# Sparse attention and a gated feed-forward on one core: 64-row value tiles with a VectorE halo copy, one cast queue in order of need, block means by row sums, score halves joined

## The chip, the core and the metric

The kernel runs on one core of one Trainium2 chip. The metric is the device time of one execution in microseconds (us). Several executions of both kernels are made alternately on the same chip. One execution is recorded by the hardware profiler. "Span" below is the time from the first to the last instruction of that recorded execution.

A ratio is the mean time of one kernel's fast runs over the mean time of the other's fast runs from the same rounds, so it is not quite the ratio of the medians that are quoted beside it. A run counts as slow when it is more than 1.5% above the fastest of the same kernel. A ratio below 1 means faster than the kernel before. A profile, and with it a span, is of one run only.

## The reference, cut to what matters

There are 4 batches, 8 heads, 768 positions and 64 values a head. Every query sees its neighbours at a distance below 16, and 24 blocks of 32 keys, each summarised by the maximum of its keys and the mean of its values. A feed-forward with a sigmoid gate follows.

```python
k_sum = k.reshape(B, H, nb, block, D).max(axis=3)        # block = 32, nb = 24
v_sum = v.reshape(B, H, nb, block, D).mean(axis=3)
scores_l = scale * q @ k.T                               # kept where |i - j| < 16
scores_s = scale * q @ k_sum.T + np.log(block)
a = softmax(concat([scores_l, scores_s]))
x = a @ concat([v, v_sum])                               # (B*S, 512) for the feed-forward
out = (sigmoid(x @ w_gate) * (x @ w_val)) @ w_out        # 512 -> 1536 -> 512
```

The kernel works in bf16 with fp32 sums.

## The kernel before

Each query tile has 64 queries. Its keys are 96 neighbours (rows 0 to 95 of a value tile) and the 24 block summaries (rows 96 to 119), so one product of 120 rows makes both parts. The value tiles of neighbouring query tiles overlap by 32 rows, and each is loaded whole:

```python
def load_v(b, t0, t1):
    for t in range(t0, t1):
        lo, hi = max(0, QT * t - 16), min(S, QT * t + 80)          # up to 96 rows
        ...
        nc.gpsimd.dma_start(out=vx_t[b % 2][r0:r0 + hi - lo, t, :, 0:64], in_=v[b, :, lo:hi, :]...)
```

For batches 0 and 1 the block means are 12 matmuls against a band of 1/32. For batches 2 and 3 they come from separately loaded block rows that GpSimd adds in halves:

```python
def V(self, *_):                                   # batches 0 and 1, on TensorE
    vsp = ps([128, 512], FP32, "vsp")
    for t in range(NQ):
        nc.tensor.matmul(out=vsp[96:128]..., lhsT=zband[:, 30 - 2 * t:62 - 2 * t],
                         rhs=vx[0:W, t, :, 0:64], start=(t == 0), stop=(t == NQ - 1))
    ...
    nc.scalar.copy(out=vx[96:120, 0, :, 0:64], in_=src)    # batch 1
    self.replicate(t0)                                     # one DMA copies it to the other tiles

def L(self, g, h=None): ...       # block rows, [96, 2048] fp32, on the sync queue
def R(self, g, h=None): ...       # GpSimd: sum of the 32 rows by halves
def M(self, g, h=None): ...       # GpSimd: times 1/32, then a small DMA into vx[96:120, 0]
```

Loads use three paths. Keys and queries of batches 0 and 1 come in fp32 on the queues of SyncE and ScalarE and are cast by an engine. Values, weights and the later batches come through GpSimd's queue, which casts while it copies. Attention work of the next batch is spread in between the feed-forward units of the current one:

```python
REST = "Q0 Q1 S0b Q2 S1b Q3 S2b S3b A0b A1b X0b A2b X1b A3b X2b X3b"
FIRST = "T0 T1 S0a S0b T2 S1a S1b T3 S2a S2b V S3a S3b"            # batch 1
LAST = "- - A0 A1 X0 A2 X1 A3 X2 X3"
spread(m1[0][1:], a0.units(REST), 2, 10)
extra = (att[1].units(FIRST) + [lambda: loads(2), lambda: means(2)]
         + att[1].units(LAST) + att[2].units(FIRST_KEYS))
spread(m1[1] + ffn.units2(), extra, 4, 23)
```

Here T and Q transpose keys and queries, S makes scores, V the block means, A the products with the values, and X transposes the result into the feed-forward's input.

The softmax here doesn't subtract the row's maximum and nothing guards it: scores larger than these inputs give would overflow.

## Time and profile before

| | kernel before |
|---|---|
| median (lowest to highest) | 256.43 us (254.42 to 256.79) |
| span of the profiled run | 251.1 us |
| TensorE, VectorE, ScalarE, GpSimd busy | 92%, 47%, 43%, 45% |
| first gapless feed-forward unit of batch 0 | 28.14 us |
| second half of batch 0's first layer | 48.17 us |
| second layer of batch 0 | 73.85 us |
| feed-forward of batch 1 | 94.01 us |

The last four rows are start times read from the engine time line; they cut the run into stages.

### The profile page before, as it was taken

To read this page: it belongs to the slowest core of one execution; us is meant where nothing else is said; L and a number is where in the kernel's file an instruction comes from. 1 tells how busy PE (TensorE), PEld (TensorE's weight loads), DVE (VectorE), ACT (ScalarE), POOL (GpSimd) and SP (SyncE) were. 2 spreads that over 40 slices of the span, in tenths; PEclk is the share of its full clock that TensorE was granted. 3 is DMA by queue.
4 is the path that set the end of the run, shared out by engine and by line. 5 is a ranking of instruction groups with operands and counts; after the bars stand their busy time and mean duration, and the time that the engine had idled before them with its cause. 6 is when DMAs were issued, how large, how long until landed. Compare 5 with 4: busy or idle time off the path is not lost.

```text
span 251.1 us, 5090 instructions
## 1 busy us (share of the span) xinstructions
PE 230.2 (92%) x2020; PEld 130.3 (52%) x2032; DVE 119.2 (47%) x243; ACT 107.8 (43%) x193; POOL 111.7 (45%) x151
## 2 busy tenths in 40 slices
PE   1696899599999999799999999999999999999993
PEld 1473566366544556455554455555544465655441
DVE  5876348247833412976563208766543034444000
ACT  2862476239943344445631134645511243333121
POOL 8998276489998389994069930000000000000000
PEclk9999999999999999999999999999999999999999
DMA  6999999999999999999999965600024310000122
GB/s 220 238 158 162 226 270 287 263 189 142 124 122 170 225 221 145 193 171 206 176 121 163 197 171 132 113 13 3 0 76 147 117 42 0 4 0 0 57 112 84
DMA packets 100687, 34.27 MB, mean 136 GB/s; under 512 B 84496, under 2 KB 97208, under 8 KB 100280
## 3 DMA queue, kind: packets, MB, share of 16 engines
q0 software_dynamic: 70720, 12.46, 65.7%
q1 hardware_dynamic: 28856, 20.70, 33.5%
q10 hardware_dynamic: 1088, 0.79, 1.0%
q8 instruction: 16, 0.26, 0.4%
q14 instruction: 7, 0.06, 0.1%
HBM read 34.34 MB, written 6.29 MB: 162 GB/s over the span
## 4 chain that ended last, share of the span: by engine, by line
PE 71%; DMA 17%; POOL 6%; issue 2%; DVE 1%; ACT 1%; SPq 0%; POOLq 0%; ACTq 0%; DVEq 0%
PE m L414 22%; PE gp L397 21%; PE vp L397 21%; DMA wv<-in_moe_w_val_dram 11%; POOL vx L166 3%; DMA kTn<-nat 3%; PE sc L257 2%; PE av L340 2%; DMA vx<-vx 2%; PE vsp L280 1%; PE tp L197 1%; POOL wg L174 1%; DVE kTx L233 1%; PE br L368 1%; POOL wv L174 1%
## 5 line engine op out<-in xcount | busy, mean ns | idle before, releaser
L405 DVE SCALAR_TENSOR_TENSOR hT<-gate,vp 128x384 bf16<-128x384 f32 x96 | 52.8, 551 | 68.9 <-PE vp L397 65.0
L397 PE MATMUL vp<-xT,wv 128*128 128x384 bf16 x384 | 78.6, 326 | 4.2 <-DMA wv<-in_moe_w_val_dram 2.7
L397 PE MATMUL gp<-xT,wg 128*128 128x384 bf16 x384 | 78.8, 327 | 1.1 <-ACT xT L371 1.1
L404 ACT ACTIVATE gate<-gp 128x384 f32<-128x384 f32 x96 | 47.4, 494 | 51.4 <-DVE hT L405 42.9
L414 PE MATMUL m<-wo,hT 128*128 128x512 bf16 x276 | 64.3, 379 | 0.6
L397 PEld LDWEIGHTS <-wv 128*128 128x128 bf16 x384 | 37.5, 98 | 30.6 <-issue 3.1
L397 PEld LDWEIGHTS <-wg 128*128 128x128 bf16 x384 | 35.3, 98 | 22.1
L414 PEld LDWEIGHTS <-hT 128*128 128x128 bf16 x288 | 26.9, 98 | 30.7
L166 POOL DMA_DIRECT2D vx<-in_v_dram x48 | 37.0, 800 | 13.1 <-PE sc L257 9.0
L419 ACT ACTIVATE ot<-m 128x512 f32<-128x512 f32 x24 | 14.3, 597 | 52.1 <-PE m L414 51.9
L263 ACT ACTIVATE P<-sc 128x768 bf16<-128x768 f32 x32 | 26.0, 815 | 12.3 <-PE sc L257 12.2
L264 DVE TENSOR_TENSOR P<-P,mask 128x768 bf16<-128x768 bf16 x32 | 17.8, 555 | 14.1 <-ACT P L263 13.9
L311 POOL TENSOR_TENSOR vm<-vm 96x1024 f32<-96x1024 f32 (+4 forms) x20 | 20.4, 1020 | 5.8 <-DMA vm<-in_v_dram 4.4
L233 DVE TENSOR_REDUCE kTx<-kTn 128x24 bf16<-128x768 bf16 x16 | 15.2, 949 | 4.5 <-ACT kTn L203 2.5
L349 DVE TENSOR_TENSOR xs<-av,rec 128x768 bf16<-128x768 f32 (+1 forms) x20 | 15.9, 797 | 0.7
L197 PE MATMUL tp<-ident,qkbf 128*128 128x128 bf16 x96 | 8.9, 253 | 6.9 <-DVE qkbf L120 5.9
L257 PEld LDWEIGHTS <-kTx 64*128 64x128 bf16 x384 | 7.9, 97 | 11.8 <-issue 8.5
L347 DVE RECIPROCAL rec<-av 128x12 f32<-128x12 f32 (+1 forms) x20 | 4.3, 215 | 19.9 <-PE av L340 19.8
L257 PE MATMUL sc<-qT,kTx 64*128 64x64 bf16 x384 | 12.0, 196 | 1.9 <-DVE kTx L237 1.2
L156 POOL DMA_DIRECT2D nat<-in_q_dram x16 | 13.2, 894 | 0.4 <-issue 0.4
L122 POOL CAST qkbf<-nat 128x768 bf16<-128x768 f32 (+1 forms) x12 | 8.5, 723 | 11.0 <-DMA nat<-in_q_dram 7.6
L156 POOL DMA_DIRECT2D nat<-in_k_dram x16 | 13.3, 852 | 0.1
(50 smaller groups left out, 114.0 us busy)
## 6 DMA issues: line engine op xcount, KB each, us to landing
out_dram<-ot SPq DMA_DIRECT2D x24, 256.0 KB, 4.6
vx<-in_v_dram POOLq DMA_DIRECT2D x40, 96.0 KB, 5.4
vm<-in_v_dram SPq DMA_DIRECT2D x4, 768.0 KB
vm<-in_k_dram SPq DMA_DIRECT2D x4, 384.0 KB, 6.9
nat<-in_k_dram SPq DMA_DIRECT2D x4, 384.0 KB
nat<-in_q_dram SPq DMA_DIRECT2D x4, 384.0 KB, 13.9
wo<-in_moe_w_out_dram POOLq DMA_DIRECT2D x6, 256.0 KB, 16.2
nat<-in_k_dram POOLq DMA_DIRECT2D x16, 96.0 KB, 4.2
```

The lines of the kernel that those rows point to most:

```text
L156: nc.gpsimd.dma_start(out=nat[:, h // 2, :, 64 * (h % 2):64 * (h % 2) + 64], in_=tap[b, h].rearrange("(c p) d -> p c d", p=128))
L166: nc.gpsimd.dma_start(out=vx_t[b % 2][r0:r0 + hi - lo, t, :, 0:64], in_=v[b, :, lo:hi, :].transpose([1, 0, 2]))
L233: nc.vector.tensor_reduce(out=kTx[:, 0, W:KX], in_=kTn[:, 16:16 + S].rearrange("p (n w) -> p n w", w=32), axis=AX.X, op=ALU.max)
L257: nc.tensor.matmul(out=sc[:, i, QT * t6:QT * (t6 + 1)], lhsT=kTx[64 * i:64 * i + 64, t, :], rhs=qT[64 * i:64 * i + 64, QT * t:QT * (t + 1) ...
L263: nc.scalar.activation(out=Ph, in_=sc[:, :, 0:6 * QT], func=ACT.Exp, scale=SCALE)
L264: nc.vector.tensor_tensor(out=Ph, in0=Ph, in1=mask[:, None, 6 * hf:6 * hf + 6, :].rearrange("p i t w -> p i (t w)") .to_broadcast([128, 2, ...
L311: nc.gpsimd.tensor_tensor(out=st[:, 0:n], in0=st[:, 0:n], in1=st[:, n:2 * n], op=ALU.add)
L349: nc.vector.tensor_tensor(out=xs[:, 0:3 * G].rearrange("p (g a) i d -> p g (a i) d", g=G), in0=avf[:, :, :, 0:64], in1=rec[:, 0:G].to_broa ...
L397: nc.tensor.matmul(out=o, lhsT=wb[:, c, 128 * f:128 * (f + 1)], rhs=self.xT[:, c, HALF * hf:HALF * (hf + 1)], start=(c == 0), stop=(c == N ...
L404: nc.scalar.activation(out=gate, in_=gp, func=ACT.Tanh, scale=0.5)
L405: nc.vector.scalar_tensor_tensor(out=self.hT[hf][:, f, :], in0=gate, scalar=1.0, in1=vp, op0=ALU.add, op1=ALU.mult)
L414: nc.tensor.matmul(out=self.m3, lhsT=self.hT[hf][:, f, 128 * tt:128 * (tt + 1)], rhs=wo_bf[:, f], start=(f == 0), stop=(f == NF - 1))
```

## The change

Its intent is to take load off the transfer engines and TensorE: value tiles of 64 rows (a third fewer bytes), the missing 32 rows copied by VectorE from the next tile; casting done by the queue, and the loads of batches 0 and 1 on one queue in the order in which they are needed, so that weights do not compete with later batches (the first-half queries of batch 0 still come in fp32 on SyncE's queue and are cast by VectorE, and the block rows of batches 2 and 3 stay on SyncE's queue too); batch 1's block means by VectorE sums of loaded rows; the near products of batch 0 taken before its block means are known; and both halves of a score pair made together.

```diff
 def load_v(b, t0, t1):
-            lo, hi = max(0, QT * t - 16), min(S, QT * t + 80)
+            lo, hi = max(0, QT * t - 16), min(S, QT * t + (48 if t < NQ - 1 else 80))
+        def halo(self, t0, t1):
+            nc.vector.tensor_copy(out=self.vx[64:96, t0:t1], in_=self.vx[0:32, t0 + 1:t1 + 1])
+        def G(self, g, h=None):                      # batch 1: row sums on VectorE
+            sm = vm_pool.tile([4 * NS, 64], FP32, name="sm", tag="sm")
+            nc.vector.tensor_reduce(out=sm, in_=st.rearrange("p (w d) -> p d w", w=32), axis=AX.X, op=ALU.add)
-        def B(self, *_):
-            self.replicate(1)                        # a DMA
+        def B(self, g, h=None):                      # VectorE
+            t0, t1 = (1, 6) if g == 0 else (6, NQ)
+            nc.vector.tensor_copy(out=self.vx[96:120, t0:t1], in_=self.vx[96:120, 0:1]...)
 ... (near, recips, far: batch 0's first half in two products)
+    load_gates((0, 1), (1, 1), (2, 2))
+    for p in range(NP):
+        srcs[0][p].append(load_qk(nc.gpsimd, q, 0, p, rows(3), half=1))
+    load_gates((4, 2), (6, 2), (8, 2), (10, 2))
+    srcs[1][0], srcs[1][1] = load_nat(1)
+    for i in range(6):
+        load_wo(i)
+    for g in range(2):
+        att[1].L(g, queue=nc.gpsimd)
+    load_v(1, 0, NQ)
 ...
+    NEXT = """
+        4 T0   5 T1   6 Z0   7 T2   8 Z1   9 T3   10 Z2   12 Z3 G0 M0   13 G1 M1   15 H0 H1   17 B0 B1
+        18 A0 A1   19 A2 A3 X0   20 X1   21 X2   22 X3"""
+    at.setdefault(4, []).append(lambda: loads(2))
+    at.setdefault(14, []).append(lambda: block_rows(2))
```

Z is both halves of a score pair, H the halo copies, G the row sums; the numbers are the feed-forward units after which the work is put out.

## The prediction

> **What bounds the kernel now.** I read the page first (shares, slices), then the chain that ended last, then the time line of the engines that it names, then the DMA queues in short windows.
>
> ```profile
> PE 230.2 (92%) x2020; PEld 130.3 (52%) x2032; DVE 119.2 (47%) x243; ACT 107.8 (43%) x193; POOL 111.7 (45%) x151
> ...
> DMA  6999999999999999999999965600024310000122
> ...
> PE 71%; DMA 17%; POOL 6%; issue 2%; DVE 1%; ACT 1%; SPq 0%; POOLq 0%; ACTq 0%; DVEq 0%
> ```
>
> TensorE is busy 92% of 251.1 us, and no other compute engine reaches half. But the DMA row (busy tenths of the 16 transfer engines) is full for nearly all of the first 23 of 40 slices, some 144 us: there are two resources to fill here, and transfers need not be late to be close to it. The third line is the chain: 23% of it lies on transfers and on GpSimd (POOL), nearly all of it early. Its longest piece, with its start and length:
>
> ```profile
> 25.31 21.82 DMA wv<-in_moe_w_val_dram
> ```
>
> The last slice of one weight, issued at 25.31, takes 21.82 us to land, and TensorE waits for it. TensorE's time line (start, length, instruction, count, in brackets the idle time before and what ended it) has the stages that the change touches:
>
> ```profile
> 28.14 0.81 PE L397 MATMUL gp<-xT,wg 128*128 128x384 bf16 x4
> ...
> 47.18 0.82 PE L397 MATMUL vp<-xT,wv 128*128 128x384 bf16 x4 [2.69 <-DMA wv<-in_moe_w_val_dram]
> ...
> 70.87 2.76 PE L280 MATMUL vsp<-vx,zband 96*32 96x512 bf16 x12
> ...
> 79.52 0.25 PE L340 MATMUL av<-vx,P 120*64 120x65 bf16 x2
> ...
> 94.01 0.81 PE L397 MATMUL gp<-xT,wg 128*128 128x384 bf16 x4
> ...
> 102.86 0.81 PE L397 MATMUL vp<-xT,wv 128*128 128x384 bf16 x4 [1.53 <-DVE hT L405]
> ```
>
> The feed-forward of batch 0 runs without gaps from 28.14, waits 2.69 us for weights, then makes block means of batch 1 by matmul (2.76 us), reaches batch 1's value products at 79.52 and batch 1's feed-forward at 94.01. From there to the end (251.1) TensorE is nearly always busy: 157.1 us. GpSimd in that time:
>
> ```profile
> 60.85 6.59 POOL L156 DMA_DIRECT2D nat<-in_k_dram  x8
> 67.37 6.63 POOL L156 DMA_DIRECT2D nat<-in_q_dram  x8
> 73.86 6.24 POOL L166 DMA_DIRECT2D vx<-in_v_dram  x8
> 80.89 3.02 POOL L166 DMA_DIRECT2D vx<-in_v_dram  x4 [0.79 <-DMA vx<-in_v_dram]
> ```
>
> Issuing the 28 loads of batch 2 holds GpSimd for 23 us, 0.83 us for a key or query load and 0.77 for a value tile, and nothing that TensorE waits for stands behind them. That last point is what the change alters.
>
> **What the Trainium skill says.** "DMA: Bandwidth & Descriptors", section "SWDGE vs HWDGE vs iDMA": a transfer that casts can only be issued from GpSimd, where software makes its descriptors. The trace agrees on the cost: every cast load takes 0.72 to 0.94 us of GpSimd, almost whatever its size (0.72 for a wo slice of 256 packets, 0.77 for a value tile of 768). Same page, "Issuing engines are not separate DMA queues": all queues share the same 16 engines, so one queue instead of three gains order and not bandwidth; the full DMA row beside three queues fits. "TensorE: Matmul & The Clock Gate", Part 1: TensorE falls to half clock after about 3.4 us of idleness and needs as much work to come back. The trace shows it at the start: 16 filler matmuls took 1.47 us at 14.6 and 1.07 us at 17.1. "VectorE: DVE Perf Modes", the tier table: a bf16 copy in SBUF moves four elements a cycle. It agrees: 1152 elements took 0.45 us at 8.5, so about 0.15 + 0.26 ns an element.
>
> **The change, TensorE's side.** (a) Batch 0 loses the fp32 casts (0.5 to 0.65 us a pair on each of VectorE and ScalarE), spreads only half of the keys, and takes its near products before the value sums are done; I put the first gapless unit at 24 instead of 28.14, -4. (b) Weights come with nothing beside them: -2.7. (c) Batch 1's sums leave TensorE: -2.8. (d) A score group alone costs 0.37 us (0.09 to switch, 0.28), a joined pair 0.55 instead of 0.74: 13 joins, -2.5, of which 8 lie after batch 1's start. (e) Added: half-width transposes in Q, +0.7. Sum about -11, so 240 if TensorE stayed the bound.
>
> **The change, the queue's side.** The order of instructions in the built kernel shows what the diff hides: on GpSimd the two multiplications that finish batch 1's block means (M0, M1) come after all loads of batch 2, because those are put out at slot 4 and the means at slots 12 and 13. VectorE's copies B0 and B1 need those means, and batch 1's products A0 (slot 18) need the copies. 98 DMA issues come before M0: keys 4, values 12, gates 14, query halves 4, batch 1 keys and queries 16, wo 6, block rows 2, values 12, then 16 and 12 of batch 2. Each also waits for the landing of the eighth before it.
>
> When does GpSimd get there? Two rates from windows that only its queue used:
>
> ```profile
> q0 software_dynamic: 1343, 0.67, 133.4%
> ...
> q0 software_dynamic: 14972, 1.88, 197.4%
> ```
>
> The first (22 to 26) is weight packets of 1,024 source bytes: 336 a us, 344 GB/s of source. The second (60 to 75) is packets of 128 bytes: 1,000 a us. Up to batch 1's block rows the queue moves 14.2 MB in large pieces (keys 1.57, queries 0.79 + 0.79, gates 6.29, wo 3.15, rows 1.57): 41 us at 344 GB/s; and 6,144 value plus 12,288 key and query packets: 18.4 us. Started at 1.8, with about 1.5 lost while the first values are bound by issue, the rows land at 63. The last four value tiles of batch 1 wait for its first four to land, so that group is issued by about 68. Then 16 x 0.83 + 12 x 0.77 = 22.5: M0 starts at 90. Floor, if nothing ever waited: 98 x 0.79 + 2.2 = 80.
>
> TensorE gets to A0 at about 71: 24 + 17.9 (28.14 to 48.17 less the wait, plus Q) + 20.0 (12 units of 1.30, four transposes of 0.68, three joined scores) + 9 (six second-product units of 1.3, one score). It then waits some 24 us. After M0: 0.4, the two small transfers 4 (two issues of 0.83, an output issue of 0.36 between them, landing about 2), B0 and B1 0.84 + 0.98 by the copy rate: A0 at 96. From A0 to batch 1's feed-forward: two products 0.8, five units of 1.3, two more products that wait for VectorE's 1.19 a pair, four transposes of 0.35: 10 us, plus about 2 at half clock. It starts at 108 instead of 94.01: +14. All of (a) to (c) is inside the wait and worth nothing.
>
> From there: 157.1, less 1.5 (the wait at 102.86, whose transposing loads now run on emptier engines), less 8 x 0.19 for joins and 0.6 for joined products, plus VectorE's burden. A hT must follow its vp within 1.95 us (three groups of 0.65) and normally takes 0.75. K (1.78) with a halo copy (0.98) in one slot makes it late by 0.8, and so do the three like slots, about 2.8 a batch in two batches; I count half. 157.1 - 3.6 + 2.8 = 156. Sum 108 + 156 = 264 us of span. The timed median was 5.5 above the profiled span: 269.5. The floor of the queue pulls down and little pulls up, so I put 266.
>
> **Rivals.** *The queue is quicker than I think.* For it: early windows moved 390 GB/s, and 64-row tiles have a third fewer packets. Against: the issue cost does not fall with size. At the floor of 80 batch 1 starts at 98, and the time is about 259. *TensorE stays the bound*: the order of GpSimd does not matter, 240 of span, about 246. For it: 92% busy, and the change takes out all its early waits. Against: this needs M0 before 65, below the floor by 15 us. *VectorE becomes the bound in batches 2 and 3*: halo and means copies are 3.6 us a batch more, and a long copy ahead of hT makes TensorE wait. Its 47% speaks against; at worst it adds 3 us to my sum, 272.
>
> **Range and chances.** M0 between 83 and 93 gives 260 to 273 by the same sum; with the early rates uncertain I take 257 to 273. Faster by 2% (below 251.5) needs batch 1 to start before about 89: 0.07. Within 2% (to 261.8) needs M0 at 82 or below, or larger joins: 0.18. Slower: 0.75.
>
> **What would show it.** Right: TensorE idle for some 15 to 25 us ahead of the first batch 1 product, ended by VectorE's copy of the means; GpSimd issuing without a pause until M0 at 85 to 92; first unit near 24 and no wait for weights; PEclk low just after the gap. Wrong: products of batch 1 before 80, or GpSimd's 98 issues done by 75, or waits of hT above 1 us in every batch.

## More of the kernel before

The kernel before took 256.43 us in the rounds of the main comparison and about 254 us on the chips of the experiments, so experiments are compared by ratio or by span.

One more row of the page, the busy tenths of 40 equal slices, serves later:

```profile
DVE  5876348247833412976563208766543034444000
```

Counted from 1, VectorE has slack in slices 5 to 9 (slice 7 apart) and 12 to 16. The row of the clock that the throttle granted has a 9 in all 40 slices.

## The result and the profile after

The changed kernel took 273.4 us median (272.51 to 274.18, 4 runs) against 256.43 us. The ratio is 1.0703, with a 95% interval of 1.0639 to 1.0767: 7% slower. The prediction had the direction and the mechanism; 273.4 is 0.4 us above its range.

From the page of the changed kernel: the shares, the granted clock (PEclk, in tenths of full speed), and the chain that ended last.

```profile
PE 236.4 (87%) x2080; PEld 133.0 (49%) x2080; DVE 141.8 (52%) x272; ACT 105.5 (39%) x186; POOL 120.5 (44%) x162
...
PEclk9999999999999966999889999999999999999999
...
PE 50%; POOL 19%; DMA 19%; issue 4%; DVE 3%; ACT 3%; SPq 1%; POOLq 0%; DVEq 0%; ACTq 0%
```

TensorE now carries 50% of the chain instead of 71%, and GpSimd 19% instead of 6%. VectorE has 22.6 us more work, and TensorE 6.2 us more. The granted clock has a hole in slices 15 and 16 (95 to 109 us), where TensorE had stood still.

TensorE's time line (start, length, instruction, count; in brackets the idle time before and what ended it), at the places that answer to those shown of before:

```profile
35.66 1.49 PE L457 MATMUL gp<-xT,wg 128*128 128x384 bf16 x4
...
82.48 1.46 PE L474 MATMUL m<-wo,hT 128*128 128x512 bf16 x6
...
84.32 7.94 PE L474 MATMUL m<-wo,hT 128*128 128x512 bf16 x36
99.79 0.29 PE L403 MATMUL av<-vx,P 120*64 120x65 bf16 x2 [7.52 <-DMA vx<-mb]
102.74 0.49 PE L403 MATMUL av<-vx,P 120*64 120x65 bf16 x10 [2.67 <-DVE vx L386]
103.64 1.21 PE L403 MATMUL av<-vx,P 120*64 120x65 bf16 x36 [0.41 <-DVE vx L386]
...
114.74 0.81 PE L457 MATMUL gp<-xT,wg 128*128 128x384 bf16 x4
```

The first gapless unit comes at 35.66 instead of 28.14, and its four matmuls take 1.49 us instead of 0.81: TensorE runs at half rate there. Done with its other work at 92.26 (84.32 + 7.94), it waits 10.6 us in three pieces for the block means of batch 1. Batch 1's feed-forward starts at 114.74 instead of 94.01. The rest takes 157.5 us (272.2 - 114.7) against 157.1 before.

| stage | before, us | after, us | difference |
|---|---|---|---|
| start to the first gapless unit | 28.14 | 35.66 | +7.5 |
| first half of batch 0's first layer | 20.03 | 22.42 | +2.4 |
| second half, with batch 1's transposes and scores | 25.68 | 24.40 | -1.3 |
| second layer of batch 0 to batch 1's feed-forward | 20.16 | 32.26 | +12.1 |
| the rest | 157.1 | 157.5 | +0.4 |

GpSimd's time line in the same run, with the row of the view of waits for the first wait:

```profile
64.45 0.68 POOL L155 DMA_DIRECT2D vx<-in_v_dram  x1 [4.15 <-DMA vm<-in_v_dram]
71.38 3.45 POOL L155 DMA_DIRECT2D vx<-in_v_dram  x5 [6.25 <-DMA vm<-in_v_dram]
...
88.00 9.09 POOL L155 DMA_DIRECT2D vx<-in_v_dram  x12
97.16 0.82 POOL L379 TENSOR_SCALAR mb<-sm 96x64 bf16<-96x64 f32 x2
```

```profile
POOL vx L155 <- DMA vm<-in_v_dram: 10.4, 2, 6.2
```

The seventh and the eighth of batch 1's value loads wait 10.4 us for the two transfers of block rows (vm) that stand ahead of them, each for the load eight places before it. Then come the 28 loads of batch 2, and only then, at 97.16, the two multiplications that the products need. VectorE in that time:

```profile
86.28 7.21 DVE L374 TENSOR_REDUCE sm<-vm 96x64 f32<-96x2048 f32 x2
93.52 1.90 DVE L316 COPY vx<-vx 32x3168 bf16<-32x3168 bf16 x2
101.17 2.42 DVE L386 COPY vx<-vx 24x2640 bf16<-24x2640 bf16 x2 [5.75 <-DMA vx<-mb]
```

The sums of the rows, 3.6 us each, end at 93.5. So GpSimd's order holds the means back by 3.7 us only: the sums are a second limit close behind the first. The sums start that late because, in VectorE's program, they stand behind the scores put out after unit 12 of batch 0 (counted from 0, the first of the second layer), and TensorE itself was late.

### The profile page after: what moved, and what is told of

Read it like the earlier page. It is cut to its first block, busy times and chain, and to the rows that moved or that the text cites. A ratio compares the mean times of both kernels' runs of the same rounds, so it can differ in the third digit from the quotient of the medians.

```text
span 272.2 us, 5243 instructions
## 1 busy us (share of the span) xinstructions
PE 236.4 (87%) x2080; PEld 133.0 (49%) x2080; DVE 141.8 (52%) x272; ACT 105.5 (39%) x186; POOL 120.5 (44%) x162
## 4 chain that ended last, share of the span: by engine, by line
PE 50%; POOL 19%; DMA 19%; issue 4%; DVE 3%; ACT 3%; SPq 1%; POOLq 0%; DVEq 0%; ACTq 0%
PE m L474 18%; PE gp L457 14%; PE vp L457 14%; DMA wv<-in_moe_w_val_dram 6%; POOL nat L145 6%; DMA vx<-in_v_dram 5%; POOL vm L367 4%; POOL vx L155 4%; DMA nat<-in_q_dram 3%; DMA qkbf<-in_k_dram 3%; DMA vm<-in_v_dram 3%; POOL wo L168 2%; DVE hT L465 2%; POOL wg L163 1%; PE sc L271 1%
## 5 line engine op out<-in xcount | busy, mean ns | idle before, releaser
L457 PE MATMUL gp<-xT,wg 128*128 128x384 bf16 x384 | 81.3, 333 | 4.0 <-DVE hT L465 2.7
L457 PE MATMUL vp<-xT,wv 128*128 128x384 bf16 x384 | 81.1, 333 | 0.0
L155 POOL DMA_DIRECT2D vx<-in_v_dram x48 | 33.7, 741 | 29.3 <-DMA vm<-in_v_dram 10.4
L277 ACT ACTIVATE P<-sc 128x768 bf16<-128x768 f32 x32 | 24.4, 808 | 9.8 <-PE sc L271 9.8
L145 POOL DMA_DIRECT2D nat<-in_k_dram x24 | 21.4, 891 | 4.2 <-DMA wg<-in_moe_w_gate_dram 2.3
L145 POOL DMA_DIRECT2D nat<-in_q_dram x24 | 20.5, 856 | 1.5 <-DMA wv<-in_moe_w_val_dram 1.0
L403 PE MATMUL av<-vx,P 120*64 120x65 bf16 x336 | 8.1, 203 | 11.0 <-DMA vx<-mb 7.5
L403 PEld LDWEIGHTS <-P 120*64 120x64 bf16 x336 | 6.8, 117 | 15.1 <-issue 13.2
L250 DVE TENSOR_REDUCE kTx<-kTn 128x24 bf16<-128x768 bf16 x12 | 11.4, 949 | 4.3 <-DMA kTn<-nat 2.9
L433 ACT COPY xT<-br 128x384 bf16<-128x384 bf16 (+1 forms) x12 | 6.9, 586 | 11.0 <-PE br L430 11.0
L271 PE MATMUL sc<-qT,kTx 64*128 64x64 bf16 x384 | 9.5, 197 | 1.5 <-DVE kTx L243 1.4
## 6 DMA issues: line engine op xcount, KB each, us to landing
vm<-in_v_dram POOLq DMA_DIRECT2D x2, 768.0 KB, 15.8
```

Of the source, the lines that this page charges most:

```text
L145: nc.gpsimd.dma_start(out=nat[:, h // 2, :, 64 * (h % 2):64 * (h % 2) + 64], in_=tap[b, h].rearrange("(c p) d -> p c d", p=128))
L271: nc.tensor.matmul(out=sc[:, i, QT * t6:QT * (t6 + 1)], lhsT=kTx[64 * i:64 * i + 64, t, :], rhs=qT[64 * i:64 * i + 64, QT * t:QT * (t + 1) ...
L277: nc.scalar.activation(out=Ph, in_=sc[:, :, 0:6 * QT], func=ACT.Exp, scale=SCALE)
L403: nc.tensor.matmul(out=av[r:r + 64, t // 6, (t % 6) // 2, i, 0:65], lhsT=P[0:KX, i, t, :], rhs=vx[0:KX, t, 2 * p + i, 0:65], start=True, s ...
L457: nc.tensor.matmul(out=o, lhsT=wb[:, c, 128 * f:128 * (f + 1)], rhs=self.xT[:, c, HALF * hf:HALF * (hf + 1)], start=(c == 0), stop=(c == N ...
```

## The experiments

Eleven kernels were run. All outputs are right. "Theory Q" below is the prediction's: the chain of GpSimd's order, multiplication, transfers and copies sets the end. Each heading is followed by the edit and what came of it.

### An earlier TensorE (`warm`)

```diff
 def U(self, p, h=None):                    # changed kernel
+    for _ in range(64 if p == 0 else 0):
+        nc.tensor.transpose(pk[:, 0:128], ident, ident)      # fillers, overwritten later
...
+    for _ in range(12 if p > 0 else 0):
+        nc.tensor.transpose(pq[:, 0:128], ident, ident)
```

> The changed kernel with 64 filler transposes before the first key transposes and 12 before each later query transpose, so that TensorE's clock is up when work arrives. Theory Q (the order on GpSimd: the first multiplication of batch 1's means, at 97.2, sets the time): the first gapless unit moves from 35.7 to about 29, the wait ahead of batch 1's products grows by as much, batch 1's feed-forward still starts at 114 +-1, the time stays 272 to 274. Rival T (TensorE was simply late, and VectorE's sums of block rows, which it starts only when TensorE gets to slot 12, hold the means): batch 1 starts 5 to 7 us earlier, time about 267.

It took 273.3 us median, ratio 1.079 (1.0713 to 1.0867). TensorE's first feed-forward matmul came at 24.92 instead of 29.98, the first gapless unit at 30.59. The time did not fall. TensorE's and GpSimd's time lines:

```profile
101.83 0.29 PE L407 MATMUL av<-vx,P 120*64 120x65 bf16 x2 [12.65 <-DMA vx<-mb]
```

```profile
99.19 0.82 POOL L383 TENSOR_SCALAR mb<-sm 96x64 bf16<-96x64 f32 x2
```

The five microseconds won at the start reappear as waiting: 12.65 instead of 7.52 us. GpSimd reached the multiplication no earlier: 2.0 us later, in fact, and batch 1's feed-forward started at 117.10, above the 114 +-1 expected. Why GpSimd was later is open. VectorE's sums were done at 90.4 (83.19 + 7.20), 8.8 us before that multiplication, so here GpSimd's order is what ends last, by far. This is what theory Q says and rival T does not. It also shows that, as long as this chain stands, the late start cost the changed kernel nothing.

### The multiplication off GpSimd (`moff`), and both together (`warm_moff`)

```diff
 def M(self, g, h=None):
-    nc.gpsimd.tensor_scalar_mul(out=mb, ...)
+    (nc.vector if self.b == 1 else nc.gpsimd).tensor_scalar_mul(out=mb, ...)
```

> The changed kernel with batch 1's two multiplications on VectorE right behind its sums instead of on GpSimd behind 28 loads. Theory Q says GpSimd is what holds the means, but VectorE's second sum ends at 93.5, so only 97.6 - 93.6 = 3.5 to 4 us can come back: time 269.5 to 270. Rival T: the same here, 3.5 or less. If the order on GpSimd cost the whole 12 us at this place, as I had predicted, the time would fall to about 262.

> Both edits. If GpSimd's order and VectorE's late sums are two limits of nearly the same length, either edit alone gives little and both together give clearly more than the sum: the sums start when TensorE gets to slot 12, some 6 us earlier, and nothing stands behind GpSimd any more: time about 263 (Theory Q and T together). If the effects only add (0 + 3.5 or 6 + 3.5), 270 or 264.

With the multiplication on VectorE the time was 271.6 us, ratio 1.0706. The wait ahead of batch 1's products did not go; VectorE holds it now:

```profile
95.77 0.25 PE L403 MATMUL av<-vx,P 120*64 120x65 bf16 x2 [3.44 <-DVE vx L316]
99.34 0.49 PE L403 MATMUL av<-vx,P 120*64 120x65 bf16 x10 [3.31 <-DVE vx L386]
```

The first wait is for the halo copy, which stands behind the sums, and the second for the copies of the means. Batch 1's feed-forward came at 111.46, 3.3 us sooner, about the 3.5 to 4 expected. The span fell by only 1.8 us, from 272.2 to 270.4: TensorE's waits for hT (what VectorE hands to the second layer) after that point rose from 2.7 to 5.2 us. By the ratio, 1.0706 against 1.0703, nothing was won, so no gain in time is shown.

With both edits two runs took 266.89 and 268.44 us and two 273.67 and 273.81. By the 1.5% rule the latter count as slow, though their granted clock (0.947 and 0.955) is hardly lower than that of the fast ones (0.955). The ratio of the fast runs is 1.0549 (1.0448 to 1.0651). The profile is of a fast run. Against `warm` it differs by the multiplication alone, and batch 1's feed-forward came at 110.02 instead of 117.10. So with TensorE early, GpSimd's order cost 7.1 us in the profiled runs; what the slow pair did is not known. The 263 us expected did not come: VectorE's halo copy and means, behind its sums, keep 8.4 us of waiting there (3.50 + 4.91).

### The sums back on TensorE (`vsum`)

```diff
-    for g in range(2):
-        att[1].L(g, queue=nc.gpsimd)                # no block rows for batch 1
+        def V(self, p, h=None):                     # 12 matmuls and one ScalarE copy, as before
+            self.sums(0, NQ)
+            nc.scalar.copy(out=self.vx[96:120, 0, :, 0:64], in_=self.vsp[96:120]...)
-... 10 Z2   12 Z3 G0 M0   13 G1 M1   15 H0 H1   17 B0 B1
+... 10 Z2   11 V0   12 Z3 H0   13 H1   14 B0   15 B1
```

> Changed kernel with batch 1's block means made on TensorE again as in the kernel before (12 sum matmuls of about 2.8 us and one ScalarE copy) in place of block rows, VectorE sums and GpSimd multiplications; everything else as changed. Theory Q (the chain rows, GpSimd's order, multiplication, transfers, copies sets the end of batch 1's products): the wait of 7.5 + 2.7 us ahead of A0 goes, A0 comes at about 92.3 + 2.8 = 95, batch 1's feed-forward at about 105 instead of 114.7, time 263 to 265 (ratio about 1.03). Rival (the late start and TensorE's low clock alone set it; the wait is only slack that something else takes up at once): batch 1's feed-forward stays at 112 or later and the time at 271 or more.

It took 264.04 us (263.78 to 266.37), ratio 1.0405 (1.0332 to 1.0478). The span fell from 272.2 to 264.7.

```profile
84.76 2.86 PE L298 MATMUL vsp<-vx,zband 64*32 64x512 bf16 x12
...
97.29 0.96 PE L408 MATMUL av<-vx,P 120*64 120x65 bf16 x48
...
107.36 0.81 PE L462 MATMUL gp<-xT,wg 128*128 128x384 bf16 x4
```

TensorE spends 2.86 us on the sums and no longer waits ahead of the products. Batch 1 starts 7.4 us sooner, which is the whole gain. The edit takes out GpSimd's part and VectorE's sums together, so it shows what the chain of the means costs as a whole: what was to save TensorE 2.8 us made it wait 10.6 us. The expected start at 105 was 2.4 us too early, because the value products had been expected at 95 and came at 97.3.

### The shape of the row transfers (`rows16`)

```diff
 def L(...):                                # batch 1 only
-    in_=v[b, 4*g:4*g+4].rearrange("h (n w) d -> n h (w d)", w=32)
+    in_=v[b, 4*g:4*g+4].rearrange("h (n w) d -> (h n) (w d)", w=32)
 def M(...):                                # four small transfers a group instead of one
+    for i in range(4):
+        nc.sync.dma_start(out=self.vx[96:120, 0, 4 * g + i, 0:64], in_=mb[24 * i:24 * i + 24])
```

> Changed kernel with batch 1's block rows put in (head, block) order, so that source and destination both have 96 rows outermost[...]; the price is eight small transfers of means instead of two (some 6 x 0.83 us on the sync queue). If the rows were late because only part of the engines carry them: they land 3 us sooner, GpSimd's wait before batch 1's values falls from 10.4 us to 5 to 7, the multiplication M0 comes at 92 to 94 instead of 97.2, and the small transfers give most of it back: time 271 to 274. Rival (the rows are late because of what is queued ahead of them, whatever their shape): GpSimd's wait stays at 9 to 11 us, M0 at 96 to 98, time 275 to 279.

The Trainium skill, page "DMA: Bandwidth & Descriptors", section "Why a DMA increments its semaphore by 16 and not by 1", says that a transfer is shared out over the largest number of engines, up to 16, that divides the outermost sizes of both sides. With 24 blocks outermost on one side and 96 rows on the other that is 12; with 96 on both it is 16. The trace fits: the median from issue to landing fell from 15.8 to 12.4 us, a factor of 1.27, where 16 over 12 is 1.33. How many engines carried each transfer was not read from the trace. From the view of waits and GpSimd's and TensorE's time lines:

```profile
POOL vx L155 <- DMA vm<-in_v_dram: 5.5, 2, 3.1
```

```profile
90.71 0.37 POOL L381 TENSOR_SCALAR mb<-sm 96x64 bf16<-96x64 f32 x1
93.58 1.81 POOL L381 TENSOR_SCALAR mb<-sm 96x64 bf16<-96x64 f32 x1 [2.50 <-DVE sm L376]
```

```profile
101.38 0.49 PE L410 MATMUL av<-vx,P 120*64 120x65 bf16 x10 [6.57 <-DVE vx L393]
```

GpSimd's wait fell from 10.4 to 5.5 us and the first multiplication came at 90.71 instead of 97.16, almost the 90 of the prediction and sooner than the 92 to 94 expected. The time was 274.4 us, ratio 1.0814 (1.074 to 1.0889): no gain. The second multiplication now waits 2.5 us for VectorE's sum, and the eight small transfers take their share. So the rows' transfer explains why GpSimd was later than predicted. VectorE's sums, and the eight transfers of the means in place of two, leave TensorE waiting there until 101.38, so that curing the rows alone won nothing.

### All repairs (`vall`), and the same without two losses of its own (`vall2`)

```diff
 def T(...):       # both sets of six transposes first, then both ScalarE copies
+# 44 and 12 fillers as above, 8 ahead of each first-half output transpose
+sk0 = load_qk(nc.sync, k, 0, 0, ...); copy("act", srcs[0][0][0], sk0)     # first keys in fp32
+# all query casts ahead of the pair loop; the sums as in vsum
```

> Changed kernel with batch 1's means on TensorE, the transposes of a pair ahead of both copies, 44 filler transposes at the start and 12 for later pairs, 8 fillers ahead of the first-half output transposes, the first key pair loaded in fp32 beside the cast queue, and the query casts ahead of the mask. Theory (three separate losses, start 7.5, chain of means 10, second transposes 3.6): first feed-forward unit at 27 to 30 instead of 35.7, batch 1's feed-forward at 92 to 97, time 249 to 256, as fast as the kernel before or faster. Rival (the single queue keeps it back: keys, weights or values land too late for an earlier start): first unit near 28 but new waits for weights of 3 us or more in batch 0's first half, batch 1's feed-forward at 100 or later, time 259 to 264.

It took 257.73 us (256.99 to 258.2), ratio 1.0147 (1.0084 to 1.0209), which leaves open whether it is 2% slower.

```profile
12.57 0.54 PE L275 MATMUL sc<-qT,kTx 64*128 64x64 bf16 x12 [3.15 <-DVE kTx L245]
...
32.03 0.81 PE L468 MATMUL gp<-xT,wg 128*128 128x384 bf16 x4
...
98.14 0.81 PE L468 MATMUL gp<-xT,wg 128*128 128x384 bf16 x4
```

The first unit came at 32.03, later than the 27 to 30 expected, and batch 1 at 98.14. No wait for weights appeared. Measured from the first unit to batch 1's feed-forward, this kernel takes 66.1 us, and the kernel before 65.9. So, apart from the start, the loss is repaired, and 3.9 us of start remain. Part of it was my own: with all query casts ahead of the first maxima on VectorE, the third cast waited for its load and TensorE waited 3.15 us for the first keys. `vall2` moved those casts between the pairs, ran the output transposes one pair further ahead, and halved the fillers ahead of each output transpose from 8 to 4:

```diff
-for p in range(NP): cast_q(p)          # all ahead
-a0.U(0); a0.U(1)
+cast_q(0); a0.U(0); cast_q(1); a0.U(1); cast_q(2); cast_q(3)
-a0.far(2); f0.m1(0, 0, 0, 1); a0.X(1, 0); a0.far(3); f0.m1(0, 0, 1, 2); a0.X(2, 0); ...
+a0.far(2); a0.X(1, 0); a0.far(3); f0.m1(0, 0, 0, 1); a0.X(2, 0); f0.m1(0, 0, 1, 2); ...
```

> The kernel of the run with all repairs, with two losses of its own mended: the query casts are no longer all ahead of the first pair's key maxima on VectorE (the third waited for its load until 10.8 us and TensorE 3.15 us for the first keys), and the output transposes run one pair further ahead of the products that use them (TensorE waited 0.57 us twice for ScalarE's copies). Theory (with batch 1's means back on TensorE only the start is left of the loss): first gapless unit at 27 to 29 instead of 32.0, batch 1's feed-forward at 93 to 95 instead of 98.1, time 252 to 255, level with the kernel before (ratio 0.99 to 1.005). Rival (the start is bound by landings or by the clock, not by these orders): first unit at 31 or later, time 257 or more.

It took 260.77 us median (254.57 for the kernel before in the same rounds), with one run at 255.34 and five from 260.69 to 263.65. Those five count as slow by the 1.5% rule, so there is no ratio. The granted clock does not tell them apart (0.971 in the fast run, 0.954 to 0.974 in the others), so I don't put this down to the state of the chip. The profile is of one of the five. The first unit came at 31.05, not at 27 to 29: TensorE ran at half rate there (0.53 us for a matmul that took 0.32 in `vall`), and whether the fewer fillers or chance did that was not separated. Batch 1 came earlier than in any other kernel built on the changed one, at 95.76, and then TensorE met a new wait. TensorE's and VectorE's time lines:

```profile
107.73 1.44 PE L468 MATMUL vp<-xT,wv 128*128 128x384 bf16 x4 [4.65 <-DVE hT L476]
```

```profile
103.61 0.95 DVE L254 TENSOR_REDUCE kTx<-kTn 128x24 bf16<-128x768 bf16 x1 [3.12 <-DMA kTn<-nat]
104.48 1.53 DVE L245 COPY kTx<-kTn 128x1152 bf16<-128x1152 bf16 x1
```

VectorE stands 3.12 us at the maxima of batch 2's keys, whose transposing loads have not landed, and the hT that the feed-forward needs stands behind them. The expectation (level with before) held in one run of six. That this wait is what the other five lost is likely but not shown: one of them was profiled, and the fast one was not.

### The joined scores alone (`join_before`)

```diff
-FIRST = "T0 T1 S0a S0b T2 S1a S1b T3 S2a S2b V S3a S3b"     # kernel before
+FIRST = "T0 T1 - Z0 T2 - Z1 T3 - Z2 V - Z3"
-... 4 K1 D2   5 S0a   6 D3 S0b B   8 K2   9 S1a   11 S1b   13 K3 ...
+... 4 K1 D2   6 Z0 D3 B   8 K2   10 Z1   12 K3   14 Z2   18 Z3   24 A0 A1 ...
```

> The kernel before with only the score halves of batches 1 to 3 joined and the products A0 A1 and A2 A3 of batches 2 and 3 put side by side. By 0.19 us a join, 12 joins, and 0.15 for each of four joined products: -2.5 to -3 us, 253.5, with nothing given back since VectorE and ScalarE stay under half busy. If joined halves make VectorE late for hT, 256 or above.

The edit also puts the products A0 A1 and A2 A3 of batches 2 and 3 side by side. It took 254.03 us, ratio 0.9936 (0.9837 to 1.0035): the same, perhaps a little faster. Two of its four runs count as slow and are left out of the ratio, and its profile is of one of these.

### Later loads held back in the kernel before (`before_late`, `before_half`, `before_half_join`)

These three look at the part of the change that orders the loads. In the kernel before, batch 1's fp32 loads were held back so that the weights land alone. A write of one element into each staging tile, placed after some units, makes the load wait.

```diff
-    for p in range(NP): ... load_qk(k, 1, p, st[0]), load_qk(q, 1, p, st[1]) ...    # at once
+    def load_batch1():
+        for p in range(NP):
+            for x in st: nc.vector.memset(x[:, 0, 0, 0:1], 0.0)
+            ... the same loads and casts ...
+    spread(m1[0][1:], a0.units(REST)[:4] + [load_batch1] + a0.units(REST)[4:], 2, 10)
```

> Kernel before with batch 1's fp32 key and query loads held back until the first half of batch 0's feed-forward is under way, so that the weights land with less beside them. Theory (contention on the 16 engines made the last weight slice late): the 2.69 us wait for wv at 47.2 falls under 0.5 us, the 21.8 us landing to 15 to 18, and the time by 1.5 to 3 us, to about 251 (ratio 0.988 to 0.995). Rival (the weights are bound by the cast queue itself, or later loads then hold batch 1 up): the wait stays above 2 us, or a new wait appears at batch 1's transposes, and the time stays within 1 us.

The wait for weights went: no matmul between 44 and 50 us waited, and batch 1 came at 92.59 instead of 94.01. Yet the time was 264.56 us. Three of the four runs count as slow, so there is no ratio, but even the fast one, 259.93, is 2.5% above the 253.62 of the kernel before. The profile is of a slow run:

```profile
105.46 1.44 PE L397 MATMUL vp<-xT,wv 128*128 128x384 bf16 x4 [5.55 <-DVE hT L405]
```

```profile
100.11 0.95 DVE L233 TENSOR_REDUCE kTx<-kTn 128x24 bf16<-128x768 bf16 x1 [2.80 <-DMA kTn<-nat]
100.98 2.76 DVE L237 COPY kTx<-kTn 128x1152 bf16<-128x1152 bf16 x1
```

It is the same place as in `vall2`: VectorE waits for batch 2's keys ahead of an hT. At 122.21 TensorE waits for another hT, 6.10 us, behind the next pair of keys, for which VectorE waited 6.90 us. The two make 11.7 us. The copy after the maxima at 100.11, 1152 elements, takes 2.76 us where it takes 0.45 otherwise; GpSimd adds block rows in that time. The Trainium skill, page "SBUF — State Buffer", section "Who interferes with whom", says that such a VectorE copy and GpSimd lock each other out for a whole instruction. Both traces agree with it: the copies took 2.76 and 1.53 us beside GpSimd's additions. So in this run the theory's gain and the rival's later loss both came, and the loss was larger.

`before_half` held back only pairs 2 and 3, and `before_half_join` added the joined scores.

```diff
+    load_batch1(0, 2)                                    # at once
+    ... a0.units(REST)[:3] + [load_rest1] + a0.units(REST)[3:] ...   # pairs 2, 3 and the values
```

> Kernel before with only the later half of batch 1's fp32 keys and queries (pairs 2 and 3) held back until three units into the first half of batch 0's feed-forward. In the run that held all back the weight wait was gone but GpSimd's casts and everything behind them came 6 us later, and TensorE stood still for 5.6 us early in batch 1. Theory (there is a point between): the wait for wv at 47.2 falls from 2.7 to under 1 us, batch 1's casts end by 54 instead of 51.7, no new wait above 1 us, time 1 to 2.5 us shorter (ratio 0.99 to 0.996). Rival (what is held back is always lost later): the ratio is 1.00 or above.

> The same with the score halves of batches 1 to 3 joined, as the change has them (by itself that gave a ratio of 0.994, interval 0.984 to 1.004). If both gains add, the ratio is 0.98 to 0.99, the time 249 to 251, faster than both kernels; if the joined halves only move a wait, it is that of the run without them, 0.99 to 1.00.

Held back by half: 255.26 us, ratio 1.0029 (0.9982 to 1.0077), nothing. The wait for weights is gone from its trace, and a wait of 2.35 us for VectorE's xs (the scaled attention output) at 46.65 has come in its place: two mask multiplications ahead of it take 3.73 us beside GpSimd's casts, where they take 1.26 in the kernel before. `join_before`, which holds nothing back, shows the same in its slow profile (4.56 us, a wait of 3.17 us for xs, none for weights), so it is not shown that holding back removed the wait. With the joined scores: 251.3 us (250.05 to 252.46), ratio 0.9884 (0.9833 to 0.9936). This is the fastest kernel, 1.2% faster than the kernel before (clear of noise) and, by the two ratios (0.9884 over 1.0703), about 8% faster than the changed one. Two lines from its TensorE time line:

```profile
47.21 1.46 PE L401 MATMUL vp<-xT,wv 128*128 128x384 bf16 x4 [2.27 <-DMA wv<-in_moe_w_val_dram]
...
95.69 0.81 PE L401 MATMUL gp<-xT,wg 128*128 128x384 bf16 x4
```

The wait for weights is still there in this run, so its removal is not what helps. Whether the joins alone would give as much is not shown: the interval of `join_before` holds this ratio too. From 95.69 to the end (248.5) it takes 152.8 us; without the joins, 157.0 (253.1 - 96.1). So joined scores and adjacent products are worth about 4 us in this kernel (the medians, 255.26 and 251.3, say the same), and no wait for an hT is left, where one of 1.04 us was.

## Why the prediction was right or wrong

**The direction and the mechanism were right.** TensorE does wait for batch 1's means, which stand behind all loads of batch 2 on GpSimd. `vsum` shows what the chain of the means costs: without it the span falls by 7.5 us. `warm` and `warm_moff` show GpSimd's order in it.

**The step that failed is "the rows land at 63 ... issued by about 68 ... M0 starts at 90".** The prediction let the block rows pass at 344 GB/s, the rate of weight packets, which makes 4.6 us for 1.57 MB, and had the last four value loads wait for the first four. The rows took 15.8 us to land (median), and it was for the rows that GpSimd waited, 10.4 us: the seventh value load could go at 64.45 and the eighth only at 71.38. So the value loads were all issued at 74.8 instead of 68. That is 6.8 of the 7.2 us by which the multiplication was late. `rows16` shows the cause of most of it: with the rows in the other order (16 engines instead of 12, by the page's rule) the wait was 5.5 us and the multiplication came at 90.7.

**The next steps were right.** The 28 loads of batch 2 were put at 22.5 us and took 22.3 (74.8 to 97.1). From the multiplication to complete means, 6.2 were put and 6.4 measured (97.16 to 103.59). From there to batch 1's feed-forward 12 were put and 11.2 measured. So batch 1 started 6.7 us after the predicted 108.

**A limit was left out.** VectorE's row sums appear nowhere in the prediction's sum. They take 7.2 us and end 3.7 us before GpSimd is ready. The claim that the order on GpSimd is what binds was therefore true by a small margin only, and that is luck: `moff` removes it, and batch 1 starts 3.3 us sooner.

**TensorE's arrival, 71, was wrong by 21 us, and it hardly mattered.** It came at 92.3. Of that, 11.7 us are the first gapless unit at 35.66 instead of 24. The first half took 22.4 us where 17.9 were put, among other things because it began at half rate (1.49 us for four matmuls) and waited 1.37 us for spread keys. The second half took 24.4 where 20.0 were put; 3.6 of these 4.4 us are four waits of 0.89 us such as this one, between a pair's two sets of transposes, where the kernel puts ScalarE's copy (the trace gives the copy as what ended three of them and a DMA for the fourth):

```profile
69.22 0.49 PE L214 MATMUL tp<-identp,nat 128*128 128x128 bf16 x6 [0.89 <-ACT kTn L215]
```

The remaining 0.8 us lie in the second layer, where the prediction counted six units ahead of slot 18 and the trace has seven (42 matmuls). The wait was thus 10.6 us instead of the 24 put. `warm` shows that 5 us of earlier arrival buy nothing. That an arrival wrong by 21 us left the end nearly right was luck, too: the wait took it up.

**The start went the wrong way.** Step (a) counted what the change removes and nothing that it adds. The first keys reach TensorE at 7.35 instead of 5.23, since they now come by the cast queue; the query transposes of three of the four pairs wait 1.1 to 1.2 us for a cast on VectorE (the line below); and TensorE stays at half rate until about 39. That the cut from 40 filler matmuls to 16 did this is not shown: in `warm`, with 100 fillers more, TensorE ran at full rate from 7.7 us and was at half rate again from about 25 to 35.

```profile
10.86 0.50 PE L227 MATMUL tq<-identp,qb 128*128 128x128 bf16 x3 [1.10 <-DVE qb L116]
```

**The other parts.** (b) was right: no wait for weights is left. (c) was right in size and wrong in value: moving the sums off TensorE is the most expensive part of the change that a run isolates (7.5 us of span, `vsum`). (d) was perhaps too small: joined scores with adjacent products are worth about 4 us after batch 1's start on top of `before_half`, where the prediction had 2.1 and, separately, 1.5 for the wait for an hT; the sum of the two, 3.6, is close. Alone, in `join_before`, they were worth 0.6%, with an interval that holds zero. VectorE's burden was put at 2.8 us. The changed kernel waits 2.7 us for hT after batch 1's start, and the rest took 157.5 where 156 were put.

**The last term.** The sum was 264 of span, and 272.2 came: 6.7 from batch 1's start and 1.5 from the rest. To that I added 5.5 us, the median less the profiled span (5.3 by the median quoted here). It compared a median with one quick run; the difference within one run is 1.7 us. It was partly cut back to 266 with the remark that "little pulls up"; that 266 is also what 264 + 1.7 gives is chance. What pulled up was the rows' transfer. In the range, too, one end was off: M0 at 83 gives 262.5 by that sum, not 260.

**The rivals.** "The queue is quicker" and "TensorE stays the bound" were refuted by M0 at 97.16. "VectorE becomes the bound in batches 2 and 3" did not come as put, but VectorE is the second limit in batch 1, for which that rival had not been considered.

## What to carry to other kernels

Work moved off the busiest engine must be followed to its end: its new engine has a program order too, and what stands ahead of it there, loads being issued for a later batch included, becomes part of the chain. When two limits lie within a few microseconds of each other, removing one shows little, so find the second before judging the first. And an earlier arrival somewhere is worth something only if what it meets next is ready as well: in `warm` that was the means, and in the slow runs of `vall2` and `before_late`, as far as their profiles tell, the keys of the batch after.

## What the Trainium skill lacked or had wrong

- "VectorE: DVE Perf Modes", the tier table, gives `tensor_reduce` the plain rate of one element a cycle and no duration. The maxima of 768 bf16 keys agree with that (0.95 us). The sum of 2048 fp32 elements a row, read 64 elements apart, took 3.6 us, some 1.6 times the 2.29 us that the table has for 2048 fp32 elements at that rate. The page "SBUF — State Buffer" does say that an access to a new 16-byte line costs extra, which here is every element, but not how much for such a sum. Whether the type or the stride does it was not separated.
- "DMA: Bandwidth & Descriptors", the table of measured sizes under "Bandwidth", has 6.15 us for 1 MB. Block rows of 768 KB behind other loads on the queue took 15.8 us from issue to landing with 12 engines and 12.4 with 16 (engine numbers by that page's rule, which the two times fit). What a queue with work ahead adds is not there.
- "TensorE: Matmul & The Clock Gate", Part 1, says that some 3.4 us of sustained work bring the full rate. In the changed kernel TensorE had no idle time above 0.7 us from 17 to 38 us and was still at half rate at the end of that time (1.49 us for four matmuls at 35.66). In `warm` it fell back to half rate at about 25 us, after 17 us at full rate, with no idle time above 0.9 us in them once the keys were in. And it differs between runs of the same instructions: of the four single units ahead of the first gapless one, the last three took 0.32 to 0.34 us a matmul in the profile of the kernel before and about 0.5 in that of `join_before` (a slow run), whose program is the same up to there; `before_half`, in a fast run, had about 0.5 as well. What decides it was not tested.
- No page says that the row of granted clock on the profile does not show this half rate: it read full speed (1.00 in the stretch from 35.66 to 58.08) while matmuls took 1.8 times as long. The durations show it. (The nearest is the warning in "TensorE: Matmul & The Clock Gate", Part 1, that clock events in traces can be unreliable.)
- No page has the wait of GpSimd's loads for the landing of the eighth load before. It held a value load for 6.25 us behind the block rows in the changed kernel. Whether the hardware or the program's bookkeeping asks for it was not settled.
